# Moving the operand differences of a seven-product second layer to VectorE, with finer pools and more staging buffers

## The chip, the core and the metric

The kernel runs on one core of a Trainium2 chip. TensorE (PE) multiplies, ScalarE (ACT) copies, rounds and applies functions, VectorE (DVE) and GpSimd (POOL) do elementwise work, and SyncE (SP) issues the transfers, one after the other in its own order. The metric is the device time of one execution in microseconds, as the median of three runs; less is better. The profile is of one further execution.

## The reference

Attention with a compressive memory is followed by a two-layer feed-forward network; all numbers are float32.

```python
# x: 2304 tokens x 512, the output of the attention, heads side by side
h = x @ w_in                                  # w_in 512 x 2048
g = h * (1.0 / (1.0 + np.exp(-1.702 * h)))    # a gelu by a sigmoid
return (g @ w_out).astype(np.float32)         # w_out 2048 x 512
```

The attention part (softmax over 576 positions in 4 batches of 8 heads, plus a read of the memory) fills the first 410 us or so and is not touched by the change.

## The kernel before

Every float32 product is made from three faster ones: an operand is split into a rounded high part and a rest, and high x high, rest x high and high x rest are added up in PSUM.

**The schedule.** The attention is laid out in slots; `step` (line 735) runs the events of a slot in the order of their priorities and then adds matmuls of the first layer (`first_moe`, line 708) until a slot's share of TensorE time is used up. The order written in the program is only a first proposal: the framework orders each engine's instructions by a simulation, and moves one forward when its inputs and its memory are free there. On the chip each engine then keeps that order.

**First layer.** The weights are 16 blocks of 128 columns of `w_in`. A block is loaded, converted from two 32-bit words per number to float32, split and kept in SBUF (`conv_in`, line 757): blocks 0 to 5 in one pool `w1a`, blocks 6 to 15 in a second one, `w1b`. The tokens come in eight chunks of up to 320. For each chunk and each block, 12 matmuls fill one PSUM bank; one slot later `keep` (line 701) copies the bank to an SBUF tile `hk`, on VectorE for even blocks and on ScalarE for odd ones, and stores it to DRAM (`gd`). After the attention is finished (line 779) the last three or so chunks run alone: this is called the tail here. In the tail `moe_ps` has two entries; for the first 20 blocks the banks are the two of `ps_m`, afterwards the six of `ps_m2`, which the conversion below also uses.

**Weights of the second layer.** `conv_pair(kk)` (line 814), called eight times in the tail, loads two blocks of `w_out` (two raw tiles `wraw` of `cnv`, which has two buffers), rescales them on ScalarE (`ws`, in a PSUM bank), finishes them on VectorE (`bits`, three operations each, into `r`), and forms four sums and differences of quarter blocks on VectorE (`sums`, into `st`). `r` and `st` have two buffers in the pool `stg`. `w_hi` rounds all seven weight combinations on ScalarE into a tile `wo` of 14 KB per partition, and `w_lo` subtracts the rounded part on GpSimd. Pairs 0 to 4 have room in `w2a` all along; pairs 5 to 7 (`w2b`, line 943) are placed on bytes that belong to the first layer's pools, after `left.close()` (line 939).

**Second layer.** It is done with seven block products in place of eight (a Strassen-Winograd form). Tokens come in three groups of 2 x 384, columns of `g` in two halves. `G[kh, th, p]` holds a piece of 128 x 768 of half `kh`, token half `th`; each of the seven products of a group has four pieces `p`, so there are 84 units. A unit is: `split` (line 874: the rounded part `oh` on ScalarE, the rest `ol` on VectorE, into one of three buffer pairs chosen by the unit's number), then `product` (line 897: 12 matmuls of 128 x 384). `split` runs two units ahead of `product`. The raw pieces are loaded from `gd` on SyncE, put through the gelu in place on ScalarE (`gelu`, line 870), and replaced in place by differences (`diff`, line 884) as the products go on. In the kernel before, two of the four kinds of difference run on GpSimd and two on VectorE:

```python
if n + 1 < len(units) and units[n + 1][1] == 0 or s == 0 and p < 3:
    diff("P", (0, 1), (0, 0), (0, 0), (p + 1) % 4)
...
elif s == 1:
    gelu(1, 0, p)
    diff("P", (1, 1), (0, 1), (0, 1), p)
elif s == 2:
    diff("V", (1, 1), (0, 0), (1, 1), p)
elif s == 4:
    diff("V", (1, 0), (1, 1), (1, 0), p)
```

After a product `after` (line 914) saves its sums from PSUM on ScalarE, or joins them with saved ones on VectorE and stores the result.

Pools stand in two stacks, left and right. A pool opened with `reuse_waits="tile"` on bytes of a closed pool is held back tile by tile, not as a whole.

Of the kernel before, what the change touches and what calls it, by code (L numbers as in the profile page):

```python
# [34 lines left out]
def tile_attention_memory_moe(ctx, tc, kq, vq, mem, zz, beta, w_in, w_out, out):  # L35
# [19 lines left out]
    w1 = [pool(left, "w1a", side="left")]  # L55
# [642 lines left out]
    def gate(ps, n, blk):  # L698
        b, a0, w = chunks[n]
        t0 = b * S + a0  # L700
        def keep():
            h = mop.tile([128, XW], F32, name="hk", bufs=3)
            copy("AV"[blk % 2 == 0], h[:, :w], ps[:, :w])
            nc.sync.dma_start(gd[blk // 2][blk % 2, :, t0:t0 + w], h[:, :w])

        at(state["slot"] + 1, 28, keep)
# [50 lines left out]
    def conv_in(blk):  # L757
        wb[blk] = w1[blk >= W0].tile([128, 2, DM], F32R, name=f"wi{blk}")
        conv_unit(None, wb[blk], w_in[blk], cnv, {"bufs": 2}, lambda: ps_x, {"tag": "ps"}, att, {"tag": f"qpt{blk % 2}", "bufs": 2})
# [8 lines left out]
    w1.append(pool(left, "w1b", side="left", reuse_waits="tile"))  # L768
# [21 lines left out]
    g00 = pool(ctx, "g00", 4, side="right", reuse_waits="tile")  # L790
# [23 lines left out]
    def conv_pair(kk):  # L814
        box = {}
        s0 = state["slot"] + 1
        raw2[kk] = [stg.tile([128, DM], F32, name=f"r{h}") for h in range(2)]
        raw2[kk].append(stg.tile([128, 4, DH], F32, name="st"))
# [26 lines left out]
        for h in range(2):  # L845
            at(s0, 5, lambda h=h: load(h))
            at(s0 + 1, 60, lambda h=h: scale(h))
            at(s0 + 1, 61, lambda h=h: bits(h))
        at(s0 + 2, 60, sums)
        if kk < EARLY:  # L850
            at(s0 + 3, 40, lambda: new_w(w2a, kk))
            at(s0 + 3, 41, lambda: w_hi(kk))
            at(s0 + 3, 42, lambda: w_lo(kk))
# [3 lines left out]
    G, ops, snap, acc, pools = {}, {}, {}, {}, {(0, 0): g00}  # L857
    NG = NT // (2 * QN)
    ORDER2 = (0, 2, 1, 5, 6, 4, 3)
# [5 lines left out]
    def load_g(gr, kh, th, p):  # L865
        t = G[kh, th, p] = pools[kh, th].tile([128, 2, QN], F32, name=f"g{kh}{th}")
        t0 = (2 * gr + th) * QN
        nc.sync.dma_start(t, gd[4 * kh + p][:, :, t0:t0 + QN].rearrange("i p t -> p i t"))
# [5 lines left out]
    def split(n):  # L874
        s, p = units[n][1:]
        src = G[(*OPERAND[ORDER2[s]], p)]
        q, kw = (opa, {}) if n % 3 == 0 else (pools["op"], {})
        h = q.tile([128, 2, QN], F32R, name="oh", **kw)
        l = q.tile([128, 2, QN], F32R, name="ol", **kw)
# [61 lines left out]
    for kh, th in ((1, 1), (1, 0)):  # L941
        pools[kh, th] = pool(ctx, f"g{kh}{th}", 4, side="left", reuse_waits="tile")
    w2b = pool(ctx, "w2b", side="left", reuse_waits="tile")
    pools[0, 1] = pool(ctx, "g01", 4, side="left", reuse_waits="tile")
    for kk in range(EARLY, KK):
        new_w(w2b, kk)
# [4 lines left out]
    pools["op"] = pool(ctx, "opb", 2, side="right", reuse_waits="tile")  # L951
    pools["ps"] = pool(ctx, "ps_a", 8, space=PSUM, side="left", reuse_waits="tile")
    for p in range(4):
        load_g(0, 1, 1, p)
        load_g(0, 0, 1, p)
# [3 lines left out]
    gelu(0, 1, 0)  # L959
    diff("P", (0, 1), (0, 0), (0, 0), 0)  # L960
    for n, (gr, s, p) in enumerate(units):
        if gr == 0 and s == 0 and p < 3:
            gelu(0, 1, p + 1)
        if n + 1 < len(units) and units[n + 1][1] == 0 or s == 0 and p < 3:
            diff("P", (0, 1), (0, 0), (0, 0), (p + 1) % 4)
        if s == 0:
            gelu(1, 1, p)
        elif s == 1:
            gelu(1, 0, p)
            diff("P", (1, 1), (0, 1), (0, 1), p)  # L970
        elif s == 2:
            diff("V", (1, 1), (0, 0), (1, 1), p)
        elif s == 4:
            diff("V", (1, 0), (1, 1), (1, 0), p)
        if n + 2 < len(units):
            split(n + 2)
        if gr + 1 < NG and s >= 4:
            load_g(gr + 1, *((0, 1), (1, 1), (1, 0))[s - 4], p)
            if s == 5:
                load_g(gr + 1, 0, 0, p)  # L980
            if s >= 5:
                gelu(0, int(s == 5), p)
# [56 lines left out]
```

## Time and profile before

| what | us |
|---|---|
| median of three runs (712.08 to 717.24) | 713.27 |
| the profiled execution, its own time | 712.18 |
| its span, first to last instruction | 710.4 |
| first matmul of the second layer | 494.4 |
| end of the last matmul | 707.0 |

TensorE is busy for 88% of the span, VectorE 68%, ScalarE 59%, GpSimd 47%; the mean granted TensorE clock is 0.969. The profiled execution counts 1.8 us more than its span. Times in the rows are from the start of the span. A releaser ("<-") is what ended an engine's wait.

### The profile page before, as it was taken

The numbers are of one execution on the slowest core, as the hardware profiler recorded it, in microseconds if no ns is written. First come the engines' busy times: TensorE is split into PE (matmuls) and PEld (weight loads), VectorE is DVE, ScalarE is ACT, GpSimd is POOL, SyncE is SP. The second block draws the span as 40 slices with busy tenths as digits, with TensorE's granted clock in tenths as the row PEclk, the third lists the DMA queues.
The fourth block names the chain that finished last, engine by engine and source line by source line (L and its number), as shares of the span: only waits on it lengthen the run. The fifth ranks groups of instructions, "written<-read, shape, count | busy, mean of one in ns | idle before, by whom it ended". The sixth has DMA issues, their size and how long they took to land. (4 is left out here: it accounts for less than half of the span.)

```text
span 710.4 us, 12508 instructions
## 1 busy us (share of the span) xinstructions
PE 622.2 (88%) x4032; PEld 588.1 (83%) x4032; DVE 485.3 (68%) x1106; ACT 421.0 (59%) x955; POOL 333.6 (47%) x335
## 2 busy tenths in 40 slices
PE   4688898799987899998999979879099997997898
PEld 3577786699976799998999968879099997997897
DVE  5887756587578757777486368871597579548944
ACT  5666547786777847775765365422835853674342
POOL 3657456975577755654852045501970063008200
PEclk9999999999999999999999999989589999999999
DMA  8859678976757776668721276554704630671001
GB/s 264 247 161 275 207 208 225 250 195 197 200 139 205 215 207 181 177 177 244 198 78 51 77 256 227 176 176 135 243 1 127 187 131 1 180 212 54 1 22 68
DMA packets 73537, 116.70 MB, mean 164 GB/s; under 512 B 8320, under 2 KB 53376, under 8 KB 73472
## 3 DMA queue, kind: packets, MB, share of 16 engines
q1 hardware_dynamic: 73472, 115.90, 55.8%
q8 instruction: 32, 0.52, 0.3%
q14 instruction: 33, 0.27, 0.1%
HBM read 63.97 MB, written 27.79 MB: 129 GB/s over the span
## 5 line engine op out<-in xcount | busy, mean ns | idle before, releaser
L91 PE MATMUL pm<-xh,wi 128*128 128x288 f32 (+2 forms) x1024 | 224.0, 307 | 21.3 <-ACT hk L100 8.8
L91 PEld LDWEIGHTS pm<-xh,wi 128*128 128x128 f32 x1024 | 169.3, 193 | 26.7 <-ACT hk L100 10.2
L909 PE MATMUL acc<-oh,wo 128*128 128x384 f32 x672 | 161.5, 341 | 17.6 <-ACT oh L100 17.6
L91 PE MATMUL pm<-xl,wi 128*128 128x288 f32 (+2 forms) x512 | 154.5, 302 | 0.1
L110 DVE TENSOR_TENSOR ol<-g,oh 128x768 fp32r<-128x768 f32 x84 | 98.7, 1182 | 61.5 <-ACT oh L100 59.2
L909 PEld LDWEIGHTS acc<-oh,wo 128*128 128x128 f32 x672 | 123.0, 192 | 18.1 <-ACT oh L100 18.1
L909 PE MATMUL acc<-ol,wo 128*128 128x384 f32 x336 | 102.1, 343 | 12.4 <-DVE ol L110 12.4
L100 ACT ACTIVATE oh<-g 128x768 fp32r<-128x768 f32 x84 | 70.3, 840 | 60.9 <-PE acc L909 59.7
L508 POOL TENSOR_SCALAR a<-a,sm,g 128x512 f32<-128x512 f32 (+3 forms) x112 | 72.7, 661 | 63.1 <-DVE sm L547 36.4
L110 POOL TENSOR_TENSOR g<-g,g 128x768 f32<-128x768 f32 x24 | 54.2, 2283 | 97.1 <-DVE ol L110 96.9
L91 PEld LDWEIGHTS pm<-xl,wi 128*128 128x128 f32 x512 | 98.9, 193 | 0.7 <-POOL xl L110 0.3
L499 DVE CUSTOM_DVE_ANT_0 ps<-ps,mask 128x256 f32<-128x256 f32 (+4 forms) x144 | 69.3, 496 | 18.3 <-PE ps L91 13.9
L91 PE MATMUL po<-e,vs 128*128 128x320 f32 (+3 forms) x416 | 76.1, 307 | 4.5 <-ACT e L100 3.7
L505 ACT ACTIVATE a<-ps,nm 128x512 f32<-128x512 f32 (+3 forms) x112 | 60.2, 539 | 31.1 <-DVE nm L499 26.3
L110 DVE TENSOR_TENSOR e<-pt,e 128x320 fp32r<-128x320 f32 (+1 forms) x120 | 56.5, 487 | 32.0 <-ACT e L100 31.3
L909 PEld LDWEIGHTS acc<-ol,wo 128*128 128x128 f32 x336 | 62.5, 192 | 15.7 <-DVE ol L110 15.7
L100 ACT ACTIVATE e<-pt 128x320 fp32r<-128x320 f32 (+4 forms) x136 | 55.7, 435 | 26.8 <-PE pt L95 15.0
L91 PEld LDWEIGHTS po<-e,vs 128*128 128x128 f32 x416 | 63.9, 192 | 9.2 <-ACT e L100 4.3
L91 PE MATMUL ps<-W 128*128 128x512 f32 (+3 forms) x224 | 58.7, 348 | 4.1 <-DVE e L110 2.3
L95 PE MATMUL pt<-ident,a 128*128 128x128 f32 x296 | 57.5, 276 | 0.2 <-ACT a L505 0.2
L100 ACT ACTIVATE hk<-pm 128x288 f32<-128x288 f32 (+2 forms) x64 | 26.0, 407 | 43.7 <-PE pm L91 40.7
L872 ACT ACTIVATE g<-g 128x768 f32<-128x768 f32 x48 | 39.7, 841 | 19.4 <-DMA g<-gd 19.4
(146 smaller groups left out, 1058.8 us busy)
## 6 DMA issues: line engine op xcount, KB each, us to landing
g<-gd SPq DMA_DIRECT2D x48, 384.0 KB, 4.0
gd<-hk SPq DMA_DIRECT2D x96, 144.0 KB, 2.3
wraw<-in_w_in_dram SPq DMA_DIRECT2D x16, 512.0 KB, 4.7
wraw<-in_w_out_dram SPq DMA_DIRECT2D x16, 512.0 KB, 4.2
kqr<-in_kq_dram SPq DMA_DIRECT2D x12, 608.0 KB, 5.2
W<-hi SPq DMA_DIRECT2D x24, 272.0 KB, 3.6
W<-loq SPq DMA_DIRECT2D x48, 128.0 KB, 3.5
W<-lok SPq DMA_DIRECT2D x32, 144.0 KB, 3.4
```

The source lines that it names most:

```text
L91: nc.tensor.matmul(out, l, r, start=start, stop=stop)
L95: nc.tensor.transpose(out, in_, idn)
L100: nc.scalar.activation(out=dst, in_=src, func=AF.Copy, **kw)
L110: (nc.vector if eng == "V" else nc.gpsimd).tensor_tensor(out=dst, in0=a, in1=b, op=op)
L499: nc.vector.tensor_tensor_reduce(out=ps, in0=ps, in1=mk, op0=ALU.add, op1=ALU.min, scale=-0.125, scalar=1e38 if j == 0 else nm[:, j - 1:j] ...
L505: nc.scalar.activation(out=a, in_=ps, func=AF.Exp, scale=-1.0, bias=nm, accum_out=sm)
L508: (nc.vector if eng == "V" else nc.gpsimd).tensor_scalar(out=a, in0=a, scalar1=r, scalar2=gcol, op0=ALU.mult, op1=ALU.mult)
L872: nc.scalar.activation(out=t, in_=t, func=AF.Gelu_apprx_sigmoid)
L909: nc.tensor.matmul(acc[b, j][:, :QN], W[2 * p + kk][:, WPART[i], sp, 128 * j:128 * j + 128], mv[:, kk], start=first and p + kk == 0 and sp ...
```

## The change

The change has six parts.

1. The second layer's products run in the order (2, 0, 1, 6, 5, 3, 4) in place of (0, 2, 1, 5, 6, 4, 3). All four kinds of difference run on VectorE, one kind to each of the products at places 1 to 4 of a group.
2. Each first-layer weight block has a pool of its own, and so do the weight tiles of pairs 5, 6 and 7. The order of the pools that come after them on the left is new: g10, g01, the three weight tiles, half of g11, a pair of split buffers, g00. The three split buffer pairs are in three pools.
3. Raw tiles of odd pairs come from `stg`, so that there are four raw buffers.
4. `bits`, `sums`, `w_hi` and `w_lo` of a pair come one slot later in the program.
5. In the tail every `hk` copy is on ScalarE.
6. Two pieces of g11, in place of the four of g00, are loaded and put through the gelu early in the tail; the loads of the next group move with the new order of products.

```diff
-    w1 = [pool(left, "w1a", side="left")]
+    w1 = [pool(left, f"w1_{k}", side="left") for k in range(W0)]
...
-            copy("AV"[blk % 2 == 0], h[:, :w], ps[:, :w])
+            copy("AV"[blk % 2 == 0 and len(moe_ps) == 1], h[:, :w], ps[:, :w])
...
-    w1.append(pool(left, "w1b", side="left", reuse_waits="tile"))
+    w1 += [pool(left, f"w1_{k}", side="left", reuse_waits="tile") for k in range(W0, NB)]
...
-    g00 = pool(ctx, "g00", 4, side="right", reuse_waits="tile")
+    g11a = pool(ctx, "g11a", 2, side="right", reuse_waits="tile")
...
-            box["raw", h] = cnv.tile([128, DM, 2], I32, name="wraw", bufs=2)
+            box["raw", h] = (cnv, stg)[kk % 2].tile([128, DM, 2], I32, name="wraw", bufs=2)
...
-            at(s0 + 1, 60, lambda h=h: scale(h))
-            at(s0 + 1, 61, lambda h=h: bits(h))
-        at(s0 + 2, 60, sums)
+            at(s0 + 2, 60, lambda h=h: scale(h))
+            at(s0 + 2, 61, lambda h=h: bits(h))
+        at(s0 + 3, 60, sums)
...
-    ORDER2 = (0, 2, 1, 5, 6, 4, 3)
+    ORDER2 = (2, 0, 1, 6, 5, 3, 4)
...
-        q, kw = (opa, {}) if n % 3 == 0 else (pools["op"], {})
+        q = pools["op", n % 3]
...
-    def diff(eng, a, b, to, p):
-        tt(eng, G[(*to, p)], G[(*a, p)], G[(*b, p)], ALU.subtract)
+    def diff(a, b, to, p):
+        tt("V", G[(*to, p)], G[(*a, p)], G[(*b, p)], ALU.subtract)
...
-        if k in (18, 19, 20, 21):
-            at(state["slot"] + 1, 5, lambda p=k - 18: load_g(0, 0, 0, p))
-            at(state["slot"] + 4, 50, lambda p=k - 18: gelu(0, 0, p))
+        if k in (18, 20):
+            at(state["slot"] + 1, 5, lambda p=(k - 18) // 2: load_g(0, 1, 1, p))
+            at(state["slot"] + 4, 50, lambda p=(k - 18) // 2: gelu(1, 1, p))
...
-    pools["snp"] = pool(ctx, "snp", side="left", reuse_waits="tile")
-    for kh, th in ((1, 1), (1, 0)):
-        pools[kh, th] = pool(ctx, f"g{kh}{th}", 4, side="left", reuse_waits="tile")
-    w2b = pool(ctx, "w2b", side="left", reuse_waits="tile")
+    pools[1, 0] = pool(ctx, "g10", 4, side="left", reuse_waits="tile")
     pools[0, 1] = pool(ctx, "g01", 4, side="left", reuse_waits="tile")
+    w2b = [pool(ctx, f"w2_{kk}", side="left", reuse_waits="tile") for kk in range(EARLY, KK)]
+    pools[1, 1] = pool(ctx, "g11b", 2, side="left", reuse_waits="tile")
+    pools["op", 1] = pool(ctx, "opb", side="left", reuse_waits="tile")
+    pools[0, 0] = pool(ctx, "g00", 4, side="left", reuse_waits="tile")
...
-    pools["op"] = pool(ctx, "opb", 2, side="right", reuse_waits="tile")
+    pools["op", 2] = pool(ctx, "opc", side="right", reuse_waits="tile")
+    pools["snp"] = pool(ctx, "snp", side="right", reuse_waits="tile")
...
+        if n + 2 < len(units):
+            split(n + 2)
+        if s == 0:
+            gelu(0, 0, p)
+        elif s == 1:
+            if gr == 0:
+                gelu(0, 1, p)
+            gelu(1, 0, p)
+            diff((0, 1), (0, 0), (0, 0), p)
+        elif s == 2:
+            diff((1, 1), (0, 1), (0, 1), p)
+        elif s == 3:
+            diff((1, 1), (0, 0), (1, 1), p)
+        elif s == 4:
+            diff((1, 0), (1, 1), (1, 0), p)
+        if gr + 1 < NG:
+            if s == 4:
+                load_g(gr + 1, 0, 1, p)
+            elif s == 5:
+                load_g(gr + 1, 1, 1, p)
+                gelu(0, 1, p)
+            elif s == 6:
+                load_g(gr + 1, 1, 0, p)
+                load_g(gr + 1, 0, 0, p)
+                gelu(1, 1, p)
```

## Rows read from the trace of the kernel before

**Rows 1.** Stretch: us, busy (count) of PE, PEld, DVE, ACT, POOL; clock, DMA share, GB/s.
```profile
416.00:494.40 78.40, 65.57 (x450) 63.26 (x450) 50.61 (x86) 32.43 (x61) 28.23 (x22) 0.93 0.58 192
...
464.00:470.00 6.00, 3.63 (x15) 3.63 (x16) 3.98 (x8) 1.92 (x4) 0.00 (x0) 0.62 0.41 138
...
494.40:514.30 19.90, 2.25 (x15) 1.94 (x13) 9.54 (x7) 16.39 (x25) 18.92 (x12) 0.63 0.76 252
514.30:520.00 5.70, 5.70 (x17) 5.29 (x18) 4.59 (x3) 1.51 (x2) 5.70 (x4) 0.50 0.00 0
...
590.00:596.00 6.00, 3.40 (x18) 3.08 (x17) 5.79 (x5) 1.27 (x2) 3.04 (x2) 0.92 0.00 1
596.00:602.00 6.00, 6.00 (x29) 6.00 (x28) 5.90 (x7) 2.96 (x5) 0.00 (x0) 0.79 0.01 3
...
494.40:707.00 212.60, 182.58 (x1010) 178.51 (x1008) 145.12 (x136) 117.40 (x161) 68.24 (x33) 0.94 0.34 104
```

**Rows 2.** TensorE's waits from 400 to 500 us: total, times, longest.
```profile
PE pm L91 <- ACT hk L100: 5.5, 4, 3.3
PE pm L91 <- DVE hk L103: 5.0, 2, 4.4
PE pm L91 <- DVE r L834: 2.1, 1, 2.1
```

**Rows 3.** TensorE's waits from 500 to 711 us: total, times, longest.
```profile
PE acc L909 <- ACT oh L100: 17.6, 1, 17.6
PE acc L909 <- DVE ol L110: 12.4, 9, 2.6
```

**Rows 4.** Timeline of ScalarE, undisturbed units: start, us, what, wait before.
```profile
539.15 0.85 ACT L100 ACTIVATE oh<-g 128x768 fp32r<-128x768 f32 x1 [1.23 <-PE acc L909]
541.23 0.85 ACT L100 ACTIVATE oh<-g 128x768 fp32r<-128x768 f32 x1 [1.23 <-PE acc L909]
```

**Rows 5.** Timeline of VectorE: GpSimd idle (first three), GpSimd subtracting (last two).
```profile
533.94 0.95 DVE L110 TENSOR_TENSOR ol<-g,oh 128x768 fp32r<-128x768 f32 x1
534.92 0.96 DVE L110 TENSOR_TENSOR g<-g,g 128x768 f32<-128x768 f32 x1
535.80 0.95 DVE L110 TENSOR_TENSOR ol<-g,oh 128x768 fp32r<-128x768 f32 x1
...
588.98 2.40 DVE L110 TENSOR_TENSOR g<-g,g 128x768 f32<-128x768 f32 x1
591.30 2.55 DVE L110 TENSOR_TENSOR ol<-g,oh 128x768 fp32r<-128x768 f32 x1
```

**Rows 6.** Timeline of GpSimd: last weight rest, differences at the first group change.
```profile
509.05 2.37 POOL L110 TENSOR_TENSOR wo<-st,wo 128x1024 fp32r<-128x1024 f32 x1
...
580.55 12.49 POOL L110 TENSOR_TENSOR g<-g,g 128x768 f32<-128x768 f32 x5 [0.89 <-DVE ol L110]
```

**Rows 7.** Tail: ScalarE's waits from 400 to 500 us, one in its timeline.
```profile
ACT ws L826 <- DMA wraw<-in_w_out_dram: 19.0, 10, 6.4
...
475.86 0.63 ACT L826 ACTIVATE ws<-wraw 128x512 f32<-128x512 f32 x1 [6.41 <-DMA wraw<-in_w_out_dram]
```

**Rows 8.** Timeline of SyncE in the tail: raw loads of the weights.
```profile
456.14 8.83 SPq L822 DMA_DIRECT2D wraw<-in_w_out_dram  x3
```

**Rows 9.** Timeline of ScalarE at the start of the second layer.
```profile
494.89 0.93 ACT L100 ACTIVATE wo<-r 128x256 fp32r<-128x256 f32 x2
...
513.41 1.56 ACT L100 ACTIVATE oh<-g 128x768 fp32r<-128x768 f32 x2
```

**Rows 10.** Groups by line: busy us, mean ns | idle before, releasers.
```profile
L110 POOL TENSOR_TENSOR g<-g,g 128x768 f32<-128x768 f32 x24 | 54.2, 2283 | 97.1 <-DVE ol L110 96.9
...
L103 DVE COPY hk<-pm 128x288 f32<-128x288 f32 (+2 forms) x64 | 29.0, 454 | 29.4 <-PE pm L91 16.6 <-DMA gd<-hk 9.7 <-ACT wo L100 1.8
L100 ACT ACTIVATE hk<-pm 128x288 f32<-128x288 f32 (+2 forms) x64 | 26.0, 407 | 43.7 <-PE pm L91 40.7 <-DMA gd<-hk 2.8
...
L110 DVE TENSOR_TENSOR p<-acc,p 128x384 f32<-128x384 f32 x6 | 3.3, 549 | 0.0
```

More of the change, by code (lines that the diff above doesn't have):

```diff
@@ L757, in conv_in @@
     def conv_in(blk):
-        wb[blk] = w1[blk >= W0].tile([128, 2, DM], F32R, name=f"wi{blk}")
+        wb[blk] = w1[blk].tile([128, 2, DM], F32R, name=f"wi{blk}")
         conv_unit(None, wb[blk], w_in[blk], cnv, {"bufs": 2}, lambda: ps_x, {"tag": "ps"}, att, {"tag": f"qpt{blk % 2}", "bufs": 2})
@@ L816, in conv_pair, with room @@
         s0 = state["slot"] + 1
-        raw2[kk] = [stg.tile([128, DM], F32, name=f"r{h}") for h in range(2)]
-        raw2[kk].append(stg.tile([128, 4, DH], F32, name="st"))
+        def room():
+            raw2[kk] = [stg.tile([128, DM], F32, name=f"r{h}") for h in range(2)]
+            raw2[kk].append(stg.tile([128, 4, DH], F32, name="st"))
+        at(s0 + 2, 59, room)
         def load(h):
-            box["raw", h] = cnv.tile([128, DM, 2], I32, name="wraw", bufs=2)
+            box["raw", h] = (cnv, stg)[kk % 2].tile([128, DM, 2], I32, name="wraw", bufs=2)
             nc.sync.dma_start(box["raw", h].rearrange("p f w -> p (f w)"), w_out[kk + KK * h].bitcast(I32))
@@ L846, in conv_pair @@
             at(s0, 5, lambda h=h: load(h))
-            at(s0 + 1, 60, lambda h=h: scale(h))
-            at(s0 + 1, 61, lambda h=h: bits(h))
-        at(s0 + 2, 60, sums)
+            at(s0 + 2, 60, lambda h=h: scale(h))
+            at(s0 + 2, 61, lambda h=h: bits(h))
+        at(s0 + 3, 60, sums)
         if kk < EARLY:
[L851 to L857, printed above, removed]
+            at(s0 + 4, 40, lambda: new_w(w2a, kk))
+            at(s0 + 4, 41, lambda: w_hi(kk))
+            at(s0 + 4, 42, lambda: w_lo(kk))
+    G, ops, snap, acc, pools = {}, {}, {}, {}, {("op", 0): opa}
     NG = NT // (2 * QN)
-    ORDER2 = (0, 2, 1, 5, 6, 4, 3)
+    ORDER2 = (2, 0, 1, 6, 5, 3, 4)
     OPERAND = {0: (0, 0), 1: (1, 0), 2: (1, 1), 3: (1, 0), 4: (0, 0), 5: (1, 1), 6: (0, 1)}
@@ L865, in load_g @@
     def load_g(gr, kh, th, p):
-        t = G[kh, th, p] = pools[kh, th].tile([128, 2, QN], F32, name=f"g{kh}{th}")
+        q = g11a if kh and th and p < 2 else pools[kh, th]
+        t = G[kh, th, p] = q.tile([128, 2, QN], F32, name=f"g{kh}{th}")
         t0 = (2 * gr + th) * QN
@@ L876, in split @@
         src = G[(*OPERAND[ORDER2[s]], p)]
-        q, kw = (opa, {}) if n % 3 == 0 else (pools["op"], {})
-        h = q.tile([128, 2, QN], F32R, name="oh", **kw)
-        l = q.tile([128, 2, QN], F32R, name="ol", **kw)
+        q = pools["op", n % 3]
+        h = q.tile([128, 2, QN], F32R, name="oh")
+        l = q.tile([128, 2, QN], F32R, name="ol")
         copy("A", h, src)
@@ L950, in tile_attention_memory_moe @@
     late.close()
-    pools["op"] = pool(ctx, "opb", 2, side="right", reuse_waits="tile")
+    pools["op", 2] = pool(ctx, "opc", side="right", reuse_waits="tile")
+    pools["snp"] = pool(ctx, "snp", side="right", reuse_waits="tile")
     pools["ps"] = pool(ctx, "ps_a", 8, space=PSUM, side="left", reuse_waits="tile")
+    for p in (2, 3):
+        load_g(0, 1, 1, p)
     for p in range(4):
-        load_g(0, 1, 1, p)
+        load_g(0, 0, 0, p)
         load_g(0, 0, 1, p)
@@ L958, in tile_attention_memory_moe @@
     split(1)
-    gelu(0, 1, 0)
-    diff("P", (0, 1), (0, 0), (0, 0), 0)
+    gelu(1, 1, 2)
+    gelu(1, 1, 3)
     for n, (gr, s, p) in enumerate(units):
[L962 to L974, printed above, removed]
         if n + 2 < len(units):
             split(n + 2)
-        if gr + 1 < NG and s >= 4:
-            load_g(gr + 1, *((0, 1), (1, 1), (1, 0))[s - 4], p)
-            if s == 5:
+        if s == 0:
[19 more added lines that the diff above has]
+                load_g(gr + 1, 1, 0, p)
                 load_g(gr + 1, 0, 0, p)
-            if s >= 5:
-                gelu(0, int(s == 5), p)
+                gelu(1, 1, p)
         product(n)
```

2 lines of the change are left out of this document (1 added, 1 removed).

## The prediction

> **What bounds the kernel now.** I read the stretches first, then TensorE's waits, then the timelines of the engines it waited for. In the second layer TensorE is the bound wherever nothing disturbs it: one unit follows the other every 541.23 - 539.15 = 2.08 us [rows 4]. The 84 units need 84 x 2.08 = 174.7 us at that pace, and the layer takes 212.6 us [rows 1]. So 37.9 us are lost there, and the views say where. One wait of 17.6 us for a rounded operand `oh` stands at the start, and nine waits for rests `ol` of VectorE make 12.4 us [rows 3]. The clock is at its lower level, 1.2 GHz, for all of the 5.7 us after the long wait (granted 0.50), and for part of the stretches after the stall at the first change of group (0.92 and 0.79) [rows 1]: that is 2.85 + 0.48 + 1.26 = 4.6 us of work not done. The other 3.3 us are about 0.3 for each of the ten waits, the refilling of the pipeline.
>
> The waits for VectorE come from GpSimd. While GpSimd is idle a rest takes 0.95 us, a difference 0.96, and a pair of them repeats every 535.80 - 533.94 = 1.86 us, less than a unit. While GpSimd subtracts, the same two take 2.40 and 2.55 us [rows 5], together 4.95 where TensorE needs 2.08. GpSimd has a run of five of its differences at the first change of group [rows 6], and one of the same kind at the start and at the second.
>
> The long wait at the start is a chain. Pair 5 is rounded on ScalarE only at 494.89, when the first layer has finished, and split(1) only at 513.41 [rows 9], after GpSimd has finished the last weight rest at 509.05 + 2.37 = 511.42 [rows 6]: its buffer lies on the bytes of `stg`. Pair 5's bytes are free much earlier by the code (blocks 1 to 4 end some 11 blocks before the layer does), yet it was placed behind everything. I take it that the shared pool was followed as a whole.
>
> In the tail TensorE waits 5.5 us for `hk` copies of ScalarE, 5.0 for those of VectorE and 2.1 for `bits` [rows 2], and the clock falls to 0.62 in one stretch, 2.3 us of work [rows 1]. Behind it is the conversion: with two raw buffers a load waits for the pair before. Three loads kept SyncE for 8.83 us [rows 8], with the stores of `hk` behind them, and ScalarE's rescaling waited 19.0 us for loads [rows 7].
>
> **The change, part by part.**
>
> *Differences.* GpSimd loses 24 differences of 2283 ns [rows 10], and VectorE gains 24 x 0.96 = 23.0 us. Per group, places 1 to 4 now hold 16 pairs: 16 x 1.86 = 29.8 us, plus two joins of 0.55 [rows 10], 30.9 us in all; TensorE needs 16 x 2.08 = 33.3. VectorE is hidden with 7% to spare. Places 0, 5 and 6 have rests alone, and up to four joins. The stretch with such pairs back to back ran at the 2.08 pitch [rows 4, 5]. If the cover goes (VectorE 8% slower), each further per cent costs 0.3 us a group. A difference is made two units before its split in program order, so the chain difference, `oh`, `ol` (0.96 + 0.85 + 0.95 = 2.8 us) fits in two units (4.2). What is late next is the operand of the following product, if a load is late: the loads of a group start at place 4 and each has about four units (8.3 us) until its gelu. Of the 12.4 us I leave 0.5, of the refills 0.5, of the clock 0.
>
> *Start of the second layer.* By the new order of pools, pair 5 lies on `cnv` and blocks 0 and 1, pair 6 on blocks 1 to 5, pair 7 on 5 to 8; the second split buffer on 10 and 11, g00 on 11 to 14. In the last chunk these come free one after the other, from about 23 us before its end (13 or 14 blocks; TensorE's 65.57 us for 450 matmuls, 0.146 each [rows 1], give at most 1.75 us a block). The chain from 494.89 to 511.42 is 16.5 us, so it fits in front of the end if each link starts when its blocks are free. Then only the first group's loads are left: g10 and g01 lie on `mop`, which the last store of `hk` holds. The transfers moved 252 GB/s on average in the stretch where twelve such loads ran [rows 1], 393 KB in 1.6 us each; eight behind the last store take 12.5 us, while g01 is wanted from place 1 on (8.3 us) and g10 from place 2 (16.6 us, less two units of lead). ScalarE has three operations a unit in place 1 of this group, 3 x 0.85 = 2.55 us, so it falls 1.9 us behind over four units. Bounds for what is left of the 17.6 + 2.85 us: nothing below, all above; I take 6 for the wait and 1 for clock and refills together, because the loads start sooner than now and the weights are no longer ahead of them.
>
> So of 37.9 us about 8 stay: a gain of 30.
>
> *Four raw buffers and the later slot.* The load of a pair no longer waits for the pair before. The later slot adds 2 slots of program order per pair, which eight overlapping pairs hide; what it costs alone is bounded by nothing and one slot at the end. The two together bear on the 5.0 + 2.1 us of waits and the 2.3 us of clock, 9.4 us. *Copies on ScalarE:* up to 24 copies of 454 ns leave VectorE, and come back as 407 ns on ScalarE [rows 10], 9.8 us on an engine that was busy 32.43 of 78.4 us in the tail; VectorE was at 50.61 [rows 1]. Two gelus and loads fewer are done early, which may take some of the 5.5 us. Against it, all copies are now behind ScalarE's waits for loads. Bounds for the tail: a gain of 5.5 + 9.4 = 14.9, a loss as in the second rival. I take 7, since the loads are the larger cause and ScalarE's share can't be told.
>
> *End.* The last product now ends with four joins in place of two: two more of 0.55 us, about 1 us later.
>
> Sum: 30 + 7 - 1 = 36 us, 710.4 - 36 = 674.4 us of span. The profiled execution counted 1.8 us more than its span and lay 1.1 us under the median, so 674.4 + 2.9 = 677.
>
> **Rivals.**
>
> *The weights still come late.* If pairs 5 to 7 are still rounded only when the first layer ends (the conversion is late, or the pools don't matter), units 0 and 1 run, and unit 2 waits for its buffer on `stg`'s bytes: 511.4, less one GpSimd difference of 2.3 that stood in that chain, plus 0.85 + 0.95, is 510.9, against 494.4 + 4.2 = 498.6. A wait of 12.3 us, 2.85 of clock, 1.5 of the rest: 16.7 us stay, the gain is 21.2 + 7 - 1 = 27.2, and the time 686. For it: no row shows these rests early. Against it: a load onto a block's own bytes is what the code arranges. Without the tail's gain it is 693.
>
> *ScalarE blocks the copies (slower).* A rescaling that waits for its load holds every copy behind it, and for the first 20 blocks TensorE has two banks. Now half the copies escape through VectorE. The longest such wait was 6.41 us and ten of sixteen made 19.0 [rows 7], 1.9 each, about one block (1.75). If half of the 16 waited as long as the longest, TensorE would lose 8 x (6.41 - 1.75) = 37 us, and with the tail's gain gone the time is 710.4 - 29 + 37 + 2.9 = 721. It decides against the change from 8 x 3.6 us of loss on, waits of 5.4 us. The Trainium skill, "TensorE: Matmul & The Clock Gate", in the section on the array's architecture, says that ScalarE and VectorE take their queue strictly first in, first out; the trace agrees (the wait of 6.41 stood in front of copies), and by that rule this rival has no way round a late load. Against it speak the two more raw buffers, which make loads earlier.
>
> *VectorE or the loads become the bound.* If places 1 to 4 run 10% slower than the pairs seen, 34.0 us stand against 33.3: 2 us in three groups. If the eight loads of place 6, at 1.6 us each, come 12.5 us long where 8.3 are at hand, 4 us at each of two changes. Together 677 + 2 + 4 = 683.
>
> *It does not do what it says.* The order of instructions comes from a simulation, and waits could move elsewhere (a copy behind a rounding that waits for a block) until nothing is left of the gain: 713, needing all 36 us back.
>
> **How the numbers follow.** The forecast as summed 0.62 (665 to 686), late weights 0.20 (686, to 693), VectorE or loads 0.08 (683), no effect 0.04 (713), ScalarE blocking 0.06 (721). A measurement here can tell about 1% from no change, 7 us. Faster by more: 0.62 + 0.20 + 0.08 = 0.90; within 1%: 0.04; slower: 0.06. The range goes down to the gains' bounds (14.9 in the tail, 36 to 37 later: 713.3 - 52 = 661) and up to late weights without the tail's gain and with late loads, 693 + 4 = 697; that leaves out the last two cases and the edges.
>
> **What would show it.** Right: no GpSimd work after the start of the second layer; no rest over 1 us there except beside the last weight rests; no waits for `ol` at the two changes of group; `wo` of pairs 5 and 6 rounded before the last block; the pitch of 2.08 kept. Wrong: a wait of over 10 us at the start with the weights' rests in front of it (first rival); waits for ScalarE's `hk` above 15 us in the tail (second); waits for `g` loads or `ol` back at the changes (third).

## The result

| | before | after |
|---|---|---|
| median, us | 713.11 (712.08 to 717.24) | 675.49 (673.71 to 679.05) |
| ratio, 95% interval | | 0.947 (0.941 to 0.953) |
| the profiled execution, its span | 712.18, 710.4 | 679.05, 677.2 |
| start of the attention's last operation on VectorE | 408.99 | 410.91 |
| first matmul of the second layer | 494.4 | 487.6 |
| start of the last matmul | 706.7 | 672.7 |

The changed kernel is 5.3% faster; 677 us was forecast. The profiled execution of it is the slowest of its four, and its attention happened to end 1.9 us later than that of the kernel before. Of the executions below, one (691.2 us, with the copies on both engines) fell in a slower state of the chip and is left out of that kernel's median and ratio.

In the profile the time comes from two places. The tail, counted from here on from the start of the attention's last operation to the second layer's first matmul, went from 85.4 to 76.7 us, the second layer from 212.3 to 185.1 us. Groups by line of the changed kernel (busy us, mean ns, idle before and its releaser):

```profile
L913 PE MATMUL acc<-oh,wo 128*128 128x384 f32 x672 | 158.5, 337 | 2.6 <-ACT oh L100 2.3
L110 DVE TENSOR_TENSOR ol<-g,oh 128x768 fp32r<-128x768 f32 x84 | 79.3, 955 | 62.9 <-ACT oh L100 62.7
L913 PE MATMUL acc<-ol,wo 128*128 128x384 f32 x336 | 99.9, 340 | 2.3 <-DVE ol L110 2.2
```

The waits for `oh` and `ol`, 17.6 and 12.4 us in [rows 3], are 2.3 and 2.2. A rest takes 0.955 us on the mean of all 84, as beside an idle GpSimd in [rows 5]; the differences of GpSimd in [rows 10] are gone. Stretches of the changed kernel (us, busy and count of PE, PEld, DVE, ACT, POOL; clock, DMA share, GB/s):

```profile
411.00:487.60 76.60, 70.13 (x501) 68.72 (x500) 60.43 (x84) 48.15 (x97) 44.05 (x32) 0.93 0.64 215
426.00:432.00 6.00, 2.43 (x11) 2.08 (x10) 5.93 (x7) 5.97 (x10) 5.90 (x5) 0.50 0.92 345
432.00:438.00 6.00, 6.00 (x33) 6.00 (x33) 5.93 (x9) 3.92 (x8) 4.04 (x3) 0.65 0.21 67
487.60:510.00 22.40, 19.12 (x104) 17.32 (x103) 12.80 (x15) 16.96 (x25) 0.00 (x0) 1.00 0.69 228
510.00:673.00 163.00, 161.36 (x908) 157.22 (x906) 113.08 (x137) 93.21 (x126) 0.00 (x0) 1.00 0.34 102
```

The second layer now runs at a granted clock of 1.00 throughout (0.94 in [rows 1]), with GpSimd idle. TensorE is busy for 161.36 of its last 163.00 us. The idle time that is left is mostly at the layer's start (19.12 of 22.40 us busy) and in the tail, where a stretch at 0.50 and 0.65 holds the longest wait for a copy. TensorE's waits in the tail, all of them:

```profile
PE pm L91 <- ACT hk L100: 6.4, 4, 3.6
```

In [rows 2] there were 12.6 us of three kinds. ScalarE's rescaling hardly waits for raw words any more (19.0 us in [rows 7]):

```profile
ACT ws L829 <- DMA wraw<-in_w_out_dram: 2.4, 3, 1.2
```

The weights of pairs 5, 6 and 7 are rounded while the first layer still runs, with its copies `hk` between them (timeline of ScalarE: start, us, what, wait before):

```profile
467.59 0.92 ACT L100 ACTIVATE wo<-r 128x256 fp32r<-128x256 f32 x2
...
472.06 0.41 ACT L100 ACTIVATE hk<-pm 128x288 f32<-128x288 f32 x1 [1.22 <-PE pm L91]
472.37 0.93 ACT L100 ACTIVATE wo<-r 128x256 fp32r<-128x256 f32 x2
...
476.80 0.41 ACT L100 ACTIVATE hk<-pm 128x288 f32<-128x288 f32 x1 [1.17 <-PE pm L91]
477.11 0.93 ACT L100 ACTIVATE wo<-r 128x256 fp32r<-128x256 f32 x2
478.07 1.06 ACT L100 ACTIVATE wo<-st 128x1024 fp32r<-128x1024 f32 x1
```

The first of these stood at 494.89 in [rows 9], behind the layer's end. GpSimd's last weight rest begins at 479.85 in place of 509.05 [rows 6]:

```profile
479.85 2.44 POOL L110 TENSOR_TENSOR wo<-st,wo 128x1024 fp32r<-128x1024 f32 x1
```

And a pair of difference and rest on VectorE, back to back, repeats every 511.29 - 509.55 = 1.74 us where a unit takes 2.08 (timeline of VectorE):

```profile
509.55 0.95 DVE L110 TENSOR_TENSOR g<-g,g 128x768 f32<-128x768 f32 x1
510.42 0.95 DVE L110 TENSOR_TENSOR ol<-g,oh 128x768 fp32r<-128x768 f32 x1
511.29 0.95 DVE L110 TENSOR_TENSOR g<-g,g 128x768 f32<-128x768 f32 x1
```

### The profile page after: what moved, and what is told of

The parts are those of the page before. It is cut to its first block, busy times and chain, and to the rows that moved or that the text cites. A ratio compares the mean times of both kernels' runs of the same rounds, so it can differ in the third digit from the quotient of the medians.

```text
span 677.2 us, 12458 instructions
## 1 busy us (share of the span) xinstructions
PE 619.3 (91%) x4032; PEld 584.9 (86%) x4032; DVE 473.1 (70%) x1108; ACT 428.3 (63%) x977; POOL 280.3 (41%) x311
## 4 chain that ended last, share of the span: by engine, by line
PE 53%; DMA 14%; DVE 13%; ACT 9%; issue 5%; POOL 2%; SPq 2%; DVEq 0%; ACTq 0%; POOLq 0%
PE pm L91 22%; PE acc L913 12%; PE po L91 8%; PE pt L95 6%; DMA g<-gd 5%; PE ps L91 5%; DMA gd<-hk 4%; DVE ol L110 2%; ACT oh L100 2%; ACT g L876 1%; DVE ps L499 1%; DMA xl<-xd 1%; DMA qr<-in_vq_dram 1%; DVE g L110 1%; POOL a L508 1%
## 5 line engine op out<-in xcount | busy, mean ns | idle before, releaser
L913 PE MATMUL acc<-oh,wo 128*128 128x384 f32 x672 | 158.5, 337 | 2.6 <-ACT oh L100 2.3
L913 PEld LDWEIGHTS acc<-oh,wo 128*128 128x128 f32 x672 | 119.9, 188 | 4.9 <-ACT oh L100 4.8
L110 DVE TENSOR_TENSOR ol<-g,oh 128x768 fp32r<-128x768 f32 x84 | 79.3, 955 | 62.9 <-ACT oh L100 62.7
L913 PE MATMUL acc<-ol,wo 128*128 128x384 f32 x336 | 99.9, 340 | 2.3 <-DVE ol L110 2.2
L91 PE MATMUL po<-e,vs 128*128 128x320 f32 (+3 forms) x416 | 77.6, 311 | 3.6 <-ACT e L100 3.2
L100 ACT ACTIVATE e<-pt 128x320 fp32r<-128x320 f32 (+4 forms) x136 | 55.8, 436 | 27.3 <-PE pt L95 15.1
L100 ACT ACTIVATE hk<-pm 128x288 f32<-128x288 f32 (+2 forms) x86 | 34.4, 407 | 42.1 <-PE pm L91 35.4
L95 PE MATMUL pt<-ident,at 128*128 128x128 f32 x160 | 41.9, 285 | 4.9 <-ACT e L100 1.3
```

The lines of the kernel that those rows point to most:

```text
L91: nc.tensor.matmul(out, l, r, start=start, stop=stop)
L95: nc.tensor.transpose(out, in_, idn)
L100: nc.scalar.activation(out=dst, in_=src, func=AF.Copy, **kw)
L110: (nc.vector if eng == "V" else nc.gpsimd).tensor_tensor(out=dst, in0=a, in1=b, op=op)
L913: nc.tensor.matmul(acc[b, j][:, :QN], W[2 * p + kk][:, WPART[i], sp, 128 * j:128 * j + 128], mv[:, kk], start=first and p + kk == 0 and sp ...
```

## The experiments

Each kernel was timed against the kernel before on the same chip. The table cuts each profiled execution as above. The second layer is counted from its first matmul to the start of its last.

| kernel | median, us | ratio to before, 95% | attention ends | tail | second layer |
|---|---|---|---|---|---|
| before | 713.1 | | 409.0 | 85.4 | 212.3 |
| after | 675.5 | 0.941 to 0.953 | 410.9 | 76.7 | 185.1 |
| after, GpSimd differences at places 1 and 2 | 697.4 | 0.967 to 0.979 | 411.3 | 77.0 | 204.2 |
| after, first-layer pools as before | 676.0 | 0.936 to 0.951 | 406.1 | 77.4 | 184.3 |
| after, both pool splits undone | 687.7 | 0.954 to 0.962 | 411.8 | 77.5 | 193.5 |
| after, weights 12 KB farther | 676.1 | 0.939 to 0.948 | 411.7 | 76.4 | 183.1 |
| after, copies on both engines | 682.3 | 0.944 to 0.959 | 408.9 | 85.9 | 181.1 |
| after, two raw buffers | 683.9 | 0.948 to 0.960 | 410.2 | 82.0 | 185.1 |
| before, all differences on VectorE | 700.8 | 0.973 to 0.983 | 411.4 | 87.4 | 197.2 |
| before, with the split pools | 706.4 | 0.978 to 0.989 | 413.1 | 87.2 | 202.4 |
| after, idle work on GpSimd | 712.3 | 0.993 to 0.998 | 412.6 | 76.9 | 219.2 |
| after, six banks from the 9th block | 678.0 | 0.942 to 0.950 | 412.5 | 76.1 | 183.6 |
| after, six banks from the 1st block | 678.1 | 0.942 to 0.952 | 407.7 | 75.8 | 185.7 |
| after, weight rests on VectorE | 678.8 | 0.946 to 0.955 | 407.4 | 76.9 | 186.1 |

The attention's end moves by 7 us between these executions (406.1 to 413.1), though no experiment edits the attention. So a single profile says more by the lengths of its last two stretches than by its span.

### The differences: undone in the changed kernel

```diff
-                diff((0, 1), (0, 0), (0, 0), p)
+                diff((0, 1), (0, 0), (0, 0), p, "P")
...
-            diff((1, 1), (0, 1), (0, 1), p)
+            diff((1, 1), (0, 1), (0, 1), p, "P")
```

> The changed kernel with two of its four kinds of difference, those at places 1 and 2 of a group, back on GpSimd (24 differences, as many as before the change). Mine (what GpSimd subtracts slows VectorE's own two-operand work, and TensorE then waits for rests): VectorE's rests beside them rise from 0.95 to about 2.5 us, waits of TensorE for rests come back by some 10 us, the time is 686 to 692. Rival (the new order of products and the earlier loads gave the gain at the changes of group, not the engine): TensorE's waits for rests stay under 4 us and the time within 4 us of 675.

Measured: 697.4 us, above the expected 686 to 692. That is 22 us more than the changed kernel by the medians and 19 by the ratios (0.973 against 0.947); the tail is as before the edit (77.0), and the second layer is 19.1 us longer. Groups by line of this kernel:

```profile
L110 DVE TENSOR_TENSOR ol<-g,oh 128x768 fp32r<-128x768 f32 x84 | 100.6, 1206 | 66.4 <-ACT oh L100 65.0
L913 PE MATMUL acc<-ol,wo 128*128 128x384 f32 x336 | 103.5, 348 | 17.3 <-DVE ol L110 17.2
L110 POOL TENSOR_TENSOR g<-g,g 128x768 f32<-128x768 f32 x24 | 57.7, 2437 | 110.7 <-DVE ol L110 94.7
```

The waits for rests are back, 17.2 us, and the mean rest is 1206 ns in place of 955. Of the 19.1 us, counted on the layer to the end of its last matmul, about 13 us are more of waits for `oh` and `ol` (17.6 against 4.5), and 6.2 us are more in which TensorE counts as busy (186.71 against 180.49), at a mean granted clock of 0.97 in place of 1.00.

### The differences: alone in the kernel before

```diff
-            diff("P", (0, 1), (0, 0), (0, 0), (p + 1) % 4)
+            diff("V", (0, 1), (0, 0), (0, 0), (p + 1) % 4)
...
-            diff("P", (1, 1), (0, 1), (0, 1), p)
+            diff("V", (1, 1), (0, 1), (0, 1), p)
```

(The single difference ahead of the loop was changed in the same way.)

> The kernel before with one thing of the change: the GpSimd differences go to VectorE, in the old order of products. If GpSimd beside VectorE was the cost, the 12.4 us of waits for the rests shrink to some 2 us: 701 to 706 us. Rival: the new order of products was needed too, since at the end of a group VectorE now has joins and differences together, or a later wait takes the gain: 709 to 716 us.

Measured: 700.8 us, ratio 0.978. TensorE's waits in the second layer of this kernel:

```profile
PE acc L909 <- ACT oh L100: 15.3, 2, 15.1
PE acc L909 <- DVE ol L110: 1.6, 3, 0.6
```

Of 12.4 us of waits for rests 1.6 stay, and the layer is 15.1 us shorter, without the new order of products. The long wait at the start, a chain through the weights, stays: it is 15.1 us in place of 17.6, so some 2.5 us of the gain are there. By the ratios (0.022 of 0.053) some two fifths of the whole gain are this edit.

### Is it the engine beside, or a late result?

GpSimd's differences stood in chains that TensorE waited for. In this kernel they stay on VectorE, and GpSimd does work that nothing reads.

```diff
+    def idle_work(n):
+        l = f32(ops[n + 2][1]).rearrange("p i t -> p (i t)")
+        nc.gpsimd.tensor_tensor(out=dead[:, 1], in0=l, in1=dead[:, 0], op=ALU.subtract)
...
             diff((0, 1), (0, 0), (0, 0), p)
+            idle_work(n)
...
             diff((1, 1), (0, 1), (0, 1), p)
+            idle_work(n)
```

> The changed kernel with work added: at places 1 and 2 of each group GpSimd makes one subtraction of 128x768 per unit (24 in all) from a split rest into a scratch tile that nothing reads; all differences stay on VectorE, so no operation of the second layer waits for GpSimd's result. If the two engines slow each other when they work at the same time, the difference and the rest of these units (1.7 to 1.9 us in a unit of 2.08 us) take some 3 us, and each of 24 units loses about 1 us: 688 to 705 us, with waits for the rests. Rival: what cost 22 us with GpSimd's differences was only that 2.3 us results stood in a chain that TensorE waits for: 674 to 679 us, rests at 0.95 us.

Measured: 712.3 us, above the range of the expectation: 37 more than the changed kernel by the medians, 35 by the ratios (0.995 against 0.947). TensorE waits 27.3 us for rests. Timeline of VectorE, then one row of GpSimd's, in this kernel:

```profile
514.53 0.94 DVE L110 TENSOR_TENSOR g<-g,g 128x768 f32<-128x768 f32 x1
515.40 2.58 DVE L110 TENSOR_TENSOR ol<-g,oh 128x768 fp32r<-128x768 f32 x1
517.91 0.95 DVE L110 TENSOR_TENSOR g<-g,g 128x768 f32<-128x768 f32 x1
518.78 2.58 DVE L110 TENSOR_TENSOR ol<-g,oh 128x768 fp32r<-128x768 f32 x1
```

```profile
514.75 2.42 POOL L893 TENSOR_TENSOR dead<-ol,dead 128x768 f32<-128x768 f32 x1 [2.70 <-DVE ol L110]
```

The difference that VectorE began at 514.53, before GpSimd's operation, takes its usual 0.94 us. The rest that it begins at 515.40, while GpSimd works from 514.75 to 517.17, ends at 517.98: 0.81 us after GpSimd. So the rest does nearly nothing until GpSimd is done. The pitch of a pair becomes 518.78 - 515.40 = 3.38 us against a unit's 2.08; at 1.30 us each, 24 units would lose 31 of the 34.1 us by which the second layer grew. The expectation, 1 us for each unit, had counted too much of it as absorbed by VectorE's spare time. The Trainium skill, "SBUF — State Buffer", in the section "SBUF: two separate sides", calls the port pair that the two engines share "an exclusive lock, not a bandwidth split": of a VectorE operation with two SBUF inputs and a GpSimd operation that reads SBUF, the one that starts first has the pair to its end, and the other waits. The trace agrees for VectorE (0.94 us when it began first, 2.58 when GpSimd did).

GpSimd is held too. The same subtraction of 128x768 takes it 1.85 us in the kernel before at a time when VectorE is idle (first row below), 2.42 us above, where it began 0.22 us behind an operation of VectorE, and 7.65 us in the first of its operations in the second group of this kernel, while VectorE makes seven two-input operations, one behind the other, at 0.95 or 0.96 us each (second row):

```profile
640.78 1.85 POOL L110 TENSOR_TENSOR g<-g,g 128x768 f32<-128x768 f32 x1 [47.74 <-DVE ol L110]
...
578.17 7.65 POOL L893 TENSOR_TENSOR dead<-ol,dead 128x768 f32<-128x768 f32 x1 [42.36 <-DVE ol L110]
```

### The weights: what brought them forward

The prediction took it that the old pools were followed as a whole and that splitting them freed the weights' bytes block by block. First, only the first-layer pools undone:

```diff
-    w1 = [pool(left, f"w1_{k}", side="left") for k in range(W0)]
+    w1 = [pool(left, "w1a", side="left")]
...
-    w1 += [pool(left, f"w1_{k}", side="left", reuse_waits="tile") for k in range(W0, NB)]
+    w1.append(pool(left, "w1b", side="left", reuse_waits="tile"))
```

> The changed kernel with the first-layer weights in two pools again (blocks 0 to 5, blocks 6 to 15), everything else as changed. Mine (a shared pool holds the tiles placed on it until its last user): pair 5 is rounded only after the last block of the first layer, TensorE waits 10 to 14 us early in the second layer, and the time is 684 to 690. Rival (waits go by the bytes of single tiles, and the new placement alone brought the weights forward): rounded 15 to 20 us before the last block as now, 675.

Measured: 676.0 us, no difference, though the expectation had 684 to 690. Timeline of ScalarE, with the copies `hk` of the last chunk, which follow each other every 1.58 us:

```profile
467.91 0.41 ACT L100 ACTIVATE hk<-pm 128x288 f32<-128x288 f32 x1 [1.22 <-PE pm L91]
468.22 0.93 ACT L100 ACTIVATE wo<-r 128x256 fp32r<-128x256 f32 x2
...
470.00 0.92 ACT L100 ACTIVATE wo<-r 128x256 fp32r<-128x256 f32 x2
...
483.71 0.41 ACT L100 ACTIVATE hk<-pm 128x288 f32<-128x288 f32 x1 [1.17 <-PE pm L91]
484.02 0.93 ACT L100 ACTIVATE wo<-r 128x256 fp32r<-128x256 f32 x2
```

The second layer's first matmul is at 483.46 here, so the copy at 483.71 is that of the last block, 15, and the one at 467.91, ten blocks earlier, that of block 5. Pairs 5 and 6 stand together right behind block 5, the last of the pool `w1a`, and pair 7 right behind block 15, the last of `w1b`. By the prediction's placement pair 5 lies on blocks 0 and 1 only, pair 6 on 1 to 5 and pair 7 on 5 to 8. By these times an old pool is followed as a whole, although the new ones were opened to be held back tile by tile. It costs nothing here because `w1a` is done some 16 us before the layer's end and pair 7 has time to spare. In the changed kernel, counted back in the same way from its last copy at 487.87, the copy at 472.06 is that of block 5 and the one at 476.80 that of block 8: there pair 6 stands behind the last block that it lies on, and pair 7 too.

So undoing the first-layer pools alone does not bring the loss back. Two things were left: the split of the weights' own pool, and the new order of the pools on the left. The next two kernels separate them. In the first, the weights' pool is one again too, in the new order:

```diff
-    w2b = [pool(ctx, f"w2_{kk}", side="left", reuse_waits="tile") for kk in range(EARLY, KK)]
+    w2b = pool(ctx, "w2b", side="left", reuse_waits="tile")
```

> The changed kernel with the old pools at both ends: two pools for the first-layer blocks and one pool for the weight tiles of pairs 5, 6 and 7; the order of the pools on the left stays the changed one. Splitting either end is enough (the undone first-layer split alone left 676.0 us): with both shared, the three weight tiles are rounded only behind the last first-layer copy again, and part of the 17.6 us start wait of the kernel before comes back, 684 to 692 us. Rival: the new order of the pools moved the weights, not their number: 674 to 678 us, the weights rounded before 480 us.

Measured: 687.7 us. Timeline of ScalarE in this kernel:

```profile
489.55 0.41 ACT L100 ACTIVATE hk<-pm 128x288 f32<-128x288 f32 x1 [1.17 <-PE pm L91]
489.86 0.93 ACT L100 ACTIVATE wo<-r 128x256 fp32r<-128x256 f32 x2
```

Pair 5 stands right behind the last copy of the first layer, as in [rows 9], and TensorE waits 7.3 us for `oh` at the start, 4.6 at the longest. The one pool of the weights now lies on blocks of both old pools, and all of it is held until the later one is done.

In the second, the pools are split and the weights lie where they lay in the kernel before:

```diff
-    w2b = [pool(ctx, f"w2_{kk}", side="left", reuse_waits="tile") for kk in range(EARLY, KK)]
     pools[1, 1] = pool(ctx, "g11b", 2, side="left", reuse_waits="tile")
     pools["op", 1] = pool(ctx, "opb", side="left", reuse_waits="tile")
+    w2b = [pool(ctx, f"w2_{kk}", side="left", reuse_waits="tile") for kk in range(EARLY, KK)]
```

> The changed kernel with half of g11 and a split buffer put ahead of the three weight tiles on the left, so that these lie 12 KB farther, on the very bytes that they have in the kernel before (pair 7 on blocks 8 to 11 in place of 5 to 8); the pools stay split. If the split did it, pairs 5 and 6 still come ahead of the last first-layer copies and only pair 7 is some 5 us later, which it has to spare: 674 to 680 us. Rival: the new order of the pools, with weights on blocks that come free sooner, did it: 684 to 692 us, with the long ScalarE wait at the start of the second layer.

Measured: 676.1 us, as the changed kernel; the last roundings of the pairs begin at 473.00, 479.69 and 483.15, all ahead of the second layer's first matmul at 488.09. With all pools split the new place gains nothing.

Last, the split alone in the kernel before (the three edits of pools, in its own order):

```diff
-    w1 = [pool(left, "w1a", side="left")]
+    w1 = [pool(left, f"w1_{k}", side="left") for k in range(W0)]
...
-    w2b = pool(ctx, "w2b", side="left", reuse_waits="tile")
+    w2b = [pool(ctx, f"w2_{kk}", side="left", reuse_waits="tile") for kk in range(EARLY, KK)]
...
```

> The kernel before with one thing of the change: a pool for each first-layer block and for each of the weight tiles of pairs 5, 6 and 7. If pools that are shared as a whole held the weights back, pair 5 is rounded before 490 us and the 17.6 us wait on ScalarE shrinks by 5 to 12 us, 700 to 708 us. Rival: the pools do nothing where loads and raw buffers are as before (pair 7's last sum waits for its raw words): 711 to 716 us.

Measured: 706.4 us, ratio 0.984. TensorE's waits in the second layer of this kernel:

```profile
PE acc L909 <- DVE ol L110: 13.5, 11, 2.9
PE acc L909 <- ACT oh L100: 3.6, 2, 2.6
```

The 17.6 us wait of [rows 3] is 3.6; the waits beside GpSimd stay. The layer is 9.9 us shorter. With the 15.1 us of the differences that makes 25.0 of the 27.2 us by which the whole change shortened it; the two were not tried together without the rest.

### The tail: copies and raw buffers

```diff
-            copy("AV"[blk % 2 == 0 and len(moe_ps) == 1], h[:, :w], ps[:, :w])
+            copy("AV"[blk % 2 == 0], h[:, :w], ps[:, :w])
```

> The changed kernel with the hk copies of the tail on VectorE and ScalarE by turns again. Mine (the loads of the raw weights were the larger cause of the tail's waits, where the copies run matters little): 673 to 679. Rival (copies behind VectorE's conversion work are what held TensorE): waits for VectorE's hk of 5 us or more come back with a stretch at the lower clock, 681 to 688. Third (ScalarE's copies are what TensorE waits for now, 6.4 us): up to 6 us faster, 668 to 672.

Measured: 682.3 us, above the expected 673 to 679 and where the rival had it. TensorE's waits in the tail of this kernel:

```profile
PE pm L91 <- ACT hk L100: 10.2, 4, 7.4
PE pm L91 <- DVE hk L103: 3.7, 4, 1.8
```

The waits for VectorE's copies that the rival spoke of are 3.7 us; those for ScalarE's grew as well, and why is not shown. The tail is 9.2 us longer in the profile; 4.0 us came back in the second layer. The intervals of the ratios overlap with the changed kernel's, and of the net loss the medians say 7 us and the ratios 3.5 (0.952 against 0.947 of 714 us). That the copies on ScalarE don't harm is shown; how much they give in all is not settled.

```diff
-            box["raw", h] = (cnv, stg)[kk % 2].tile([128, DM, 2], I32, name="wraw", bufs=2)
+            box["raw", h] = cnv.tile([128, DM, 2], I32, name="wraw", bufs=2)
```

> The changed kernel with only two raw buffers for the second layer's weights (all in the one pool, as before the change). Mine: a load waits for the pair before again, ScalarE's rescaling waits 15 us or more for loads instead of 2.4, copies stand behind it, the time is 680 to 686. Rival (the later slot and the copies gave the tail's gain): 675.

Measured: 683.9 us. ScalarE's wait for raw words in the tail is back, then TensorE's wait:

```profile
ACT ws L829 <- DMA wraw<-in_w_out_dram: 15.3, 9, 3.9
```

```profile
PE pm L91 <- ACT hk L100: 11.5, 10, 4.7
```

This is the chain that the second rival feared, late words in front of copies in ScalarE's queue; the two more buffers are what keeps it away. The tail is 5.3 us longer. Here too the intervals touch (0.948 to 0.960 against 0.941 to 0.953): 8 us by the medians, 5 by the ratios.

### Three tries for a faster version

What was left in the tail was the 6.4 us of waits for copies, with the lower clock around the longest of them. That one ran from 427.01 to 430.58 (TensorE's timeline, then ScalarE's):

```profile
430.58 0.85 PE L91 MATMUL pm<-xh,wi 128*128 128x288 f32 x2 [3.57 <-ACT hk L100]
```

```profile
427.06 1.28 ACT L876 ACT_TABLE_LOAD   x1
428.35 1.58 ACT L876 ACTIVATE g<-g 128x768 f32<-128x768 f32 x2
...
430.14 0.39 ACT L100 ACTIVATE hk<-pm 128x288 f32<-128x288 f32 x1
```

The copy stood behind the early gelu, its table load and a rounding, not behind late words. The clock had fallen already before that wait began, and behind one of 2.21 us that ended at 424.77 (stretches of the changed kernel):

```profile
424.00:426.00 2.00, 1.23 (x9) 1.23 (x10) 2.00 (x6) 1.27 (x4) 2.00 (x3) 1.00 1.08 393
426.00:427.00 1.00, 1.00 (x5) 0.66 (x3) 1.00 (x2) 1.00 (x1) 1.00 (x2) 0.51 1.05 425
...
430.58:436.25 5.67, 5.67 (x23) 5.67 (x24) 5.57 (x7) 4.49 (x8) 3.96 (x4) 0.50 0.41 142
436.25:438.00 1.75, 1.75 (x15) 1.75 (x15) 1.75 (x4) 0.85 (x2) 1.40 (x2) 1.00 0.10 4
```

More banks for TensorE at that point (`LATE` 8, and 0 in the other kernel):

```diff
-    LATE = 20
+    LATE = 8
```

> The changed kernel with one constant changed: the first layer takes six more PSUM banks from its 9th block after the attention on, in place of the 21st. In the changed kernel TensorE waits 6.4 us for ScalarE's copies in the tail, 3.6 us of it behind the early gelu and its table load, and a stretch of some 12 us at a granted clock of 0.50 to 0.65 follows. With more banks free at that point the copies can be late without a wait: 668 to 673 us. Rival: the banks are then taken from the conversion of the second layer's weights, which uses the same pool, and the weights come later: 676 to 684 us.

> As the run with the six banks from the 9th block, but from the first block after the attention: if banks alone matter, as good or up to 1 us better, 667 to 673 us. Rival: the conversion of the first pairs, which shares these banks, is pushed back, and the second layer starts later: 676 to 684 us.

Measured: 678.0 and 678.1 us, no gain: the times of the rivals, but not by their mechanism. The weights are not later (second layer 183.6 and 185.7 us). With 0, a wait of 4.6 us for a copy stays at the old place (until 427.76). With 8, the stretch from 426 to 432 is free of waits, but one of 4.43 us comes 10 us later (TensorE's timeline, then the stretch):

```profile
440.76 0.85 PE L91 MATMUL pm<-xh,wi 128*128 128x288 f32 x2 [4.43 <-ACT hk L100]
```

```profile
426.00:432.00 6.00, 5.99 (x46) 5.76 (x45) 5.86 (x8) 5.94 (x10) 6.00 (x7) 1.00 0.95 348
```

Last, GpSimd's weight rests, since it slows VectorE's sums in the tail as well:

```diff
-            sub("P", lo, src, hi)
+            sub("V", lo, src, hi)
```

> The changed kernel with one more thing taken from GpSimd: the 24 rests of the second layer's weights (37.4 us of GpSimd in the tail of the changed kernel) go to VectorE. Theory: what GpSimd does to VectorE in the second layer it also does in the tail, where 32 sums of 128x256 take 29.7 us, though the fastest take 0.42 us (13.4 us in all). VectorE would save up to 16 us there and get some 16 us of rests (24 at 0.3 to 1.1 us), so its load stays, while each result is there sooner and ScalarE waits less for the sums: 668 to 674 us. Rival: VectorE is full in parts of the tail already (12.0 of 12.0 us at 438 to 450), and a rest now waits in its queue for a rounding on ScalarE and holds up the sums behind it: 676 to 684 us.

Measured: 678.8 us, no gain and in the rival's range, though the theory was right about the sums. One of the four kinds of sum, in the tail of the changed kernel and then of this one:

```profile
L110 DVE TENSOR_TENSOR st<-r,st 128x256 f32<-128x256 f32 x8 | 8.8, 1106 | 0.1
```

```profile
L110 DVE TENSOR_TENSOR st<-r,st 128x256 f32<-128x256 f32 x8 | 3.3, 418 | 0.0
```

The sums fall from 1106 to 418 ns, but VectorE has the rests in their place (19.2 us), and TensorE still waits 6.8 us for copies on ScalarE. All three tails are 75.8 to 76.9 us long. What sets that length stays open; none of these kernels beats the changed one.

## Why the prediction was right, point by point

- **The sum.** Second layer +27.2, tail +8.7, end -0.8, and -1.9 for an attention that ended later make 33.2 us, the 710.4 - 677.2 of the two profiles. Forecast were 30, 7 and -1. That the median came within 1.5 us of 677 is partly luck: the layer fell short by 2.8 us and the tail went over by 1.7, the four executions lie 5.3 us apart, and within the layer two errors partly cancelled (see what is left in it).
- **Differences.** The cause was right: the edit alone gains 15.1 us in the layer of the kernel before, and idle work on GpSimd costs 34.1. Two units behind each change of group one short wait of TensorE for a rest is left, 0.24 us (at 557.58) and 0.22 us (at 618.38), where none was forecast. The pairs ran at 1.74 us in place of the 1.86 read from [rows 5], where the difference began 0.98 us behind the rest and so was not back to back; the spare time was larger than the 7% counted.
- **Start of the second layer.** Of 17.6 + 2.85 us, 7 were left in the sum; in the layer's first 22.4 us TensorE is idle for 3.3. The chain of roundings did fit in front of the first layer's end (467.59 to 479.85 + 2.44). The reason "the shared pool was followed as a whole" fits the timelines: with the first layer's pools shared, each pair is rounded behind the last block of the old pool under it, not behind its own. What the prediction, and the expectation of that run, had wrong is what that costs: pairs 5 and 6 lie on `w1a`, which is done ten blocks before the end, so that sharing on this side alone costs no time (676.0 us), and only the one pool of the weights on both old ones does (687.7). The split of the first layer's pools alone was not tried. The loads of g01 and g10, feared as the rest of the wait, cost at most the 5.0 us that the start lost (next point).
- **What is left in the layer.** It is 185.4 - 174.7 = 10.7 us where 8 were forecast. Only 4.9 us are idle time of the matmuls. The waits of the weight loads (PEld), one of which stands ahead of each matmul, show nearly all of it:

```profile
PEld acc L913 <- DVE ol L110: 5.6, 11, 1.4
PEld acc L913 <- ACT oh L100: 4.8, 7, 1.8
```

These are 10.4 us at 18 places where an operand came late; the matmuls show 4.5 us of them, some 0.3 us less at each place, which is what the prediction counted for each wait as the refilling of the pipeline. Up to 510 us they are 5.0 us, where 7 were left for the start; behind it 5.4, where 0.5 of waits and 0.5 of refills were left. That second term was too small; why these operands come late is not shown.

- **Tail.** 8.7 us for 7. The step "the loads are the larger cause" is not shown: undone alone, the buffers lengthen the tail by 5.3 us and the copies by 9.2, but by the ratios of whole executions the buffers are worth 5 us and the copies 3.5. The two overlap in the tail, since together they would make 14.5.
- **End.** Four joins in place of two: 4.5 us from the last matmul's start to the end, 3.7 before, so 0.8 for 1.
- **Not told apart.** The new order of products, the later slot of the conversion and the early pieces of g11 were not undone one by one. The old order of products with all differences on VectorE left 1.6 us of waits for rests, so the order was not needed for that.
- **The rivals.** Late weights came true only in the kernel with both splits undone: its layer is 8.4 us longer than the changed kernel's, where the rival's price was 9 (686 against 677), but with 7.3 us of waits for `oh` in place of one of 12.3. VectorE as the bound did not come: it is full for stretches (10.00 of 10.00 us from 510 to 520), yet TensorE is busy for 9.94 of the same 10. Copies held up in ScalarE's queue are what the tail's 6.4 us are, far from the 37 of that rival, and the longest of them stood behind ScalarE's own work, not behind a load.

## What to carry to other kernels

Before an elementwise operation is put on GpSimd, look at what VectorE does at that time: if both read two SBUF operands, as here, the time of the one is added to that of the other (3.38 us for a pair that takes 1.74 alone), and VectorE does the work itself in less (0.95 us against GpSimd's 1.85). Where tiles of the next stage lie on bytes of the last one, see which pools lie under each other as a whole: here a new pool waited for the last use of every old pool under it. Give tiles that are wanted early a pool of their own, and look in the timeline for the operation behind which the first write to them stands. Read a gain by the lengths of the stages, not by the span, when a stage that nobody touched moves by several microseconds.

## What the runs showed of the hardware

- A two-input operation of VectorE that begins while GpSimd subtracts ends about 0.8 us after GpSimd does (2.58 us in place of 0.94); one that began earlier is not slowed (0.94).
- GpSimd's subtraction of 128x768 takes 1.85 us beside an idle VectorE, 2.42 us when it begins 0.22 us behind a two-input operation of VectorE, and took 7.65 us beside seven of them that followed each other.
- Not every operation of VectorE is held: the three operations of `bits`, with at most one operand in SBUF and one in PSUM, take 678 to 691 ns on the mean in the changed kernel's tail, where GpSimd is busy for 44 of 77 us, and 679 to 694 ns with the rests moved away from it (7.3 us of GpSimd). The sums, with both operands in SBUF, take 595 to 1151 ns there against 416 to 499.
- In the tail of the changed kernel the granted clock went from 1.00 (2.4 GHz) to 0.50 (1.2 GHz) at 426.0, 1.2 us after a wait of 2.2 us had ended and a microsecond before the longest wait (3.6 us). It was back at 1.00 from 436.25 on, when TensorE had been busy for 5.67 us without a gap.
